# Seven VectorE operations of each parameter chain, and one product of modulations, moved to GpSimd

## The chip, the core and the metric

The kernel runs on one core of a Trainium2 chip. A core has five engines that work side by side, each through its own instructions in order: TensorE (PE, with its weight loads PEld), VectorE (DVE), ScalarE (ACT), GpSimd (POOL) and SyncE (SP, which here only issues DMA transfers; POOL issues a few too). They wait for each other by semaphores. The metric is the device time of one execution in microseconds, lower is better.

## What is computed

The reference is one block with adaptive layer norms: an S4D convolution over 2048 tokens, then a token-mixing MLP, each behind a modulated layer norm. What matters here is the S4D kernel and the modulation:

```python
dt = jnp.exp(log_dt)
A = -jnp.exp(log_A_real) + 1j * A_imag          # (D, N) = (448, 256)
C = (C_real + 1j * C_imag) * dt[:, None]
P = jnp.exp((A * dt[:, None])[:, :, None] * pos[None, None, :])
K = 2.0 * jnp.einsum("dn,dnl->dl", C, P).real   # (448, 2048)
y = irfft(rfft(u) * rfft(K))[:L]; return y + u * D_skip
...
mod = (silu(c) @ w_mod).reshape(1, 6, 1, -1)
sa, ca, ga, sb, cb, gb = (mod[:, k] for k in range(6))
h = layernorm(x) * (1 + ca) + sa
x = x + ga * S4D(h);  h = layernorm(x) * (1 + cb) + sb;  x = x + gb * MLP(h)
```

## The kernel before

**Steps.** The 448 channels go in 28 groups of 16, each group in two halves of N; one half of one group is a *step* s = 0 to 55. In a step PE makes phases (`st_phase`, line L603, into the PSUM tiles xe and xg), ACT takes absolute values and four sines of them (`st_abs` L640 and L641, `st_step` L650 to L653), GpSimd multiplies magnitudes by sines into G (L655, L656) and makes m for the step after the next (`st_mag2`, L630 and L632), DVE makes E (L657, L658, L662, L663; L662 and L663 read PSUM for the last time and so let PE's next phases go), and PE multiplies G and E into the convolution kernel (`st_kgen`, L686). Every eight steps (`BATCH`) a *window* makes the exponentials of the next eight steps at once (L614), so that ACT's tables change seldom. The order of PE, ACT, DVE and POOL is the order in which the Python code issues: there is no reordering by a scheduler.

**Work put between.** Each step calls `between()` once in its DVE work: after L658 in most steps, after L663 in steps 8 to 15 and from 32 on. It flushes held-back DVE work (L532 and L564, products out of PSUM for the transform of u), takes layer-norm statistics of x in steps 2 to 7 (`u_stats`, L503), and advances the parameter chains by `pace[s]` = 2 pieces (`more`). In the windows `more` advances them by the numbers in WPACE.

**Parameter chains.** The parameters A, C and dt are 448x256; they are prepared 128 rows at a time. The first 128 are made before the loop (`first_chain`). The rows after them are the generators `chain(q)`, q = 1, 2, 3 (the last with 64 rows): each `yield` ends a piece. The first pieces form from |C_real|/2 and |C_imag|/2 (on ACT, into xa and ya): the sum s, the difference ya, a floor under s, the reciprocal of s (into xa), the quotient ya*xa, and s scaled up where it is tiny (t, s). Then the chain yields "logs" until the next window has taken logarithms and the arctangent on ACT (`logs`, `angle`). With two pieces a step, the first pieces of chain 1 lie in steps 0 to 3, of chain 2 in 8 to 11, of chain 3 in 16 to 19; the pieces behind the logarithms lie in the windows at s = 8 and 16, and for chain 3 in the window at 24 and the steps after.

**Modulation.** mod[0] to mod[5] come from PE (L490, weights wm) and ACT (L494). In step 9 mod[0] is multiplied by mod[2] (L1070); L564 reads it from step 16 on. x and three of the weights wm are loaded by DMAs that POOL issues (L301 in steps 0 and 1, L326 in steps 2, 3 and 5), and stand in its order.

**After the steps.** From s = 32 on the pieces of the inverse transform run beside the steps; from about 404 us on two matrix products of the MLP (L1327 to L1329, L1396 to L1398) keep PE busy to the end.

Of the kernel before, what the change touches and what calls it, by code (L numbers as in the profile page):

```python
# [15 lines left out]
ALU = mybir.AluOpType  # L16
# [209 lines left out]
def tile_adaln_s4d_mixer(ctx, tc, i, out):  # L226
# [12 lines left out]
    mod = [None] * 3 + [cp.tile([P, D], F32, name=f"mod{k}") for k in range(3, 6)]  # L239
# [7 lines left out]
    with ExitStack() as es:  # L247
        V, S, G, T = nc.vector, nc.scalar, nc.gpsimd, nc.tensor
        tt, ts, stt = V.tensor_tensor, V.tensor_scalar, V.scalar_tensor_tensor
# [118 lines left out]
        def flush(todo):  # L368
            while todo:
                todo.pop(0)()  # L370

        def chain(q):


            n = min(P, D - P * q)
            cr, ci, a, aim = (raws[q][nm][0:n] for nm in ("A_C_real", "A_C_imag", "A_log_A_real", "A_A_imag"))
            xa, ya, s, t, u, ph, p64 = (
                qp.tile([P, N], F32, tag=nm, name=nm)[0:n] for nm in ("xa", "ya", "s", "t", "u", "ph", "p64")
            )

            def split(src, places):
                hl = qp.tile([P, 2, N], F32R, tag="hl", name="hl", bufs=3)[0:n]
                V.tensor_copy(hl[:, 0], src)
                yield
                tt(hl[:, 1], src, hl[:, 0].bitcast(F32), ALU.subtract)
                for k, v in places:
                    nc.sync.dma_start(pars[q][v, k, 0:n], hl.bitcast(F32))
                yield


            S.activation(xa, cr, AF.Abs, scale=0.5)
            S.activation(ya, ci, AF.Abs, scale=0.5)
            tt(s, xa, ya, ALU.add)
            yield
            tt(ya, ya, xa, ALU.subtract)
            yield
            ts(s, s, 2.0**-120, None, ALU.max)
            yield
            V.reciprocal(xa, s)
            yield  # L400
            tt(ya, ya, xa, ALU.mult)
            yield

            ts(t, s, 2.0**-40, 2.0**80, ALU.is_lt, ALU.mult)
            yield
            stt(s, t, 1.0, s, ALU.max, ALU.mult)
            yield
            tmp[q] = a, s, u, xa, ya
            while q in tmp:
                yield "logs"  # L410
            ya = u
            yield from split(a, [(0, 1), (1, 1)])
            stt(s, t, -80 * math.log(2.0) / 2.0**80, s, ALU.mult, ALU.add)
            yield
            stt(s, ya, 0.5, s, ALU.mult, ALU.add)
            yield
            ts(s, s, ldt2[0:n, q : q + 1], None, ALU.add)
            yield
            yield from split(s, [(2, 1)])
            yield "exponents"  # L420

            ts(ph, aim, dt4[0:n, q : q + 1], None, ALU.mult)
            yield
            ts(u, ph, MAGIC, MAGIC, ALU.add, ALU.subtract)
            yield
            tt(ph, ph, u, ALU.subtract)
            yield
            yield from split(ph, [(0, 0)])

            ts(u, ph, 128.0, MAGIC, ALU.mult, ALU.add)  # L430
            yield
            ts(u, u, MAGIC, None, ALU.subtract)
            yield
            stt(p64, ph, 128.0, u, ALU.mult, ALU.subtract)
            yield
            yield from split(p64, [(1, 0)])

            ts(xa, xa, 4 * i2p, -0.5, ALU.mult, ALU.add)
            yield
            ts(u, cr, 0.0, 0.5, ALU.is_ge, ALU.subtract)  # L440
            yield
            tt(xa, xa, u, ALU.mult)
            yield
            ts(u, ci, 0.0, 0.5, ALU.is_ge, ALU.subtract)
            yield
            stt(xa, xa, 0.5, u, ALU.add, ALU.mult)
            yield
            stt(xa, ph, 63.0, xa, ALU.mult, ALU.add)
            yield
            ts(u, xa, MAGIC, MAGIC, ALU.add, ALU.subtract)  # L450
            yield
            tt(xa, xa, u, ALU.subtract)
            yield
            yield from split(xa, [(2, 0)])
# [140 lines left out]
        def load(g, exps):  # L595
            load_up(g, exps)
            load_lo(g, exps)
# [445 lines left out]
        for s in range(tail):  # L1043
            if s == 32:
                early.close()
                fp = es.enter_context(tc.tile_pool(name="fp", bufs=2, reuse_waits="tile"))
                m2p.append(right("m2l", BATCH - 3))
                yks[1] = fp.tile([P, 32, DC], F32, name="yk1", bufs=1)
                for n in range(3):
                    pc_load(n)  # L1050
                t0 = fp.tile([P, 2, P], F32, name="t0", bufs=1)
                nc.sync.dma_start(t0, i["T0"].rearrange("p (j m) -> p j m", j=2))
            if s % 2 == 0 and 0 < s and s // 2 + 2 < NG:
                load(s // 2 + 2, False)
            if s == 8:
                first.close()
            if s in late:
                late[s]()
            if s < NHALF and s % BATCH == 0:
                window(s)  # L1060
                if s == 0:
                    gp_ = right("gp", 3)
            if s % BATCH == 4:
                for g in range(s // 2 + 2, min(s // 2 + 6, NG)):
                    load(g, True)

            def between():
                flush(dve)
                if s == 9:
                    tt(mod[0], mod[0], mod[2], ALU.mult)  # L1070
                if 2 <= s < BATCH:
                    for r in range(2 * s, 2 * s + 2):
                        u_stats(r)
                if s < len(pace):
                    more(pace[s])

            mellow()
            if s // BATCH == 1 or s >= NHALF:
                flush(dve)
            if s >= NHALF:  # L1080
                flush(late_act)
                flush(dve)
                mellow()
            else:
                st_abs(s)
                flush(late_act)
                if s < 32 and s % BATCH > 1:
                    st_kgen(s - 2)
                if s % BATCH == 0:
                    if s == 16:  # L1090
                        for k in (4, 5):
                            modulation(k, 0, 1)
                    elif s == 24:
                        some(u_cols, cols, 3)
                    elif s >= 32:
                        piece(False)
                if (s + 1) % BATCH:
                    st_phase(s + 1)
                elif s + 1 < NHALF:
                    st_exponents(s + 1)  # L1100

                if s > 32 and s % BATCH:
                    st_kgen(s - 1)
                st_step(s, between)
            flush(act)
            if s == NHALF:
                st_kgen(s - 1)


            if s < 2:  # L1110
                x_load(4 + 4 * s, 4 + 4 * s, G)
            free = s > 7 and not st_s1(s % BATCH == BATCH - 1)
            if s + 2 < 32 and (s + 2) % BATCH > 1:
                st_mag2(s + 2)

            if 1 < s < 8:
                modulation(s // 2, s % 2)
            if s == 7:
                par_load(2)

            if 8 <= s < 16 and free:
                some(u_rows, rows, 1)
            if s == 12:
                par_load(3)
            if s == 16:
                spec.close()
                up = early.enter_context(tc.tile_pool(name="up", bufs=3, reuse_waits="tile"))
                for n in range(4):
                    u_load(n)
            if 17 <= s < 32 and free:  # L1130
                some(u_cols, cols, 2 if s < 24 else 3)
            if s == 31:
                flush(dve)
                flush(act)
            if s > 32:
                go = pieces[0] < NP and (s % 2 == 1 or s >= NHALF)
                piece(go, None, go or s >= NHALF)
            if s == 34:

                for t in (ft, b1, b2):  # L1140
                    V.memset(t, 0.0)
                nc.sync.dma_start(ft, i["FT"])
                nc.sync.dma_start(b1, i["B_b1"].rearrange("(t p) -> p t", p=P))
                nc.sync.dma_start(b2, i["B_b2"].rearrange("(t p) -> p t", p=P))
# [164 lines left out]
    with ExitStack() as es:  # L1309
        es.enter_context(tc.manual_schedule(engines={ENG.PE, ENG.Activation, ENG.DVE, ENG.Pool}))  # L1310
        V, S, G = nc.vector, nc.scalar, nc.gpsimd
# [118 lines left out]
```

## Time and profile before

| | |
|---|---|
| median of 3 runs | 704.5 us (704.37 to 705.57) |
| the profiled execution | 708.1 us, span 705.8 us |
| busy share of the span | PE 88%, PEld 65%, DVE 65%, ACT 62%, POOL 39% |
| instructions of DVE and POOL | 877 and 326 |
| granted TensorE clock, mean | 0.956 |

The page's rows of groups give line, engine, operation, output and input names, shape and count, then busy us in total, mean ns of one, and the idle time of the engine just before them with what ended it. Timeline rows give start and length in us, engine, line and names; in brackets stands the idle time before, and what ended it. The profile of the span lists what an engine did; its waits are inferred from semaphores.

### The profile page before, as it was taken

What the parts mean: (1) busy time and instruction counts of PE and PEld (TensorE: products, weight loads), DVE (VectorE), ACT (ScalarE), POOL (GpSimd) and SP (SyncE); (2) the same over time, 40 slices, a digit from 0 to 9 for tenths busy, and PEclk for the clock granted to TensorE, in tenths of its full rate; (3) what the DMA queues carried; (4) which work ended last, traced back from release to release, by engine and by line L of the source; (5) the groups of instructions that cost most, each with busy time, mean ns of one, the idle gap of its engine ahead of it and who ended that gap; (6) DMA issues with size and microseconds to landing.
All of it is one profiled execution on the core that took longest, in us unless ns stands there. A gap on an engine that the chain in (4) does not pass through costs nothing. (4 is left out here: it accounts for less than half of the span.)

```text
span 705.8 us, 18228 instructions
## 1 busy us (share of the span) xinstructions
PE 620.8 (88%) x7164; PEld 459.6 (65%) x7164; DVE 456.3 (65%) x877; ACT 437.6 (62%) x876; POOL 271.8 (39%) x326
## 2 busy tenths in 40 slices
PE   0759878899988879788988879999999999999997
PEld 0435445445435556565665647778999999999996
DVE  7579899889678487794864468777622263344441
ACT  5838698889887799998862558878422242222220
POOL 6487468268267778887755500000000000000000
PEclk9988999999998899998898999999999999999999
DMA  7795555568795435444246889994674445555540
GB/s 173 212 186 144 200 169 171 192 214 254 236 298 171 123 77 164 122 136 139 79 125 222 256 229 249 240 203 128 186 228 138 143 130 158 157 156 157 170 130 27
DMA packets 104051, 121.69 MB, mean 172 GB/s; under 512 B 12730, under 2 KB 91758, under 8 KB 103838
## 3 DMA queue, kind: packets, MB, share of 16 engines
q1 hardware_dynamic: 102430, 113.66, 56.1%
q0 software_dynamic: 1536, 6.87, 4.4%
q8 instruction: 57, 0.93, 0.6%
q14 instruction: 28, 0.23, 0.1%
HBM read 85.14 MB, written 34.87 MB: 170 GB/s over the span
## 5 line engine op out<-in xcount | busy, mean ns | idle before, releaser
L211 ACT CAST whi<-w 128x896 fp32r<-128x896 f32 x64 | 59.9, 940 | 139.4 <-PE o L1397 84.6
L655 POOL TENSOR_TENSOR G<-mag,gs 128x512 f32<-128x512 f32 x56 | 72.0, 1285 | 76.3 <-ACT gs L651 76.3
L220 DVE TENSOR_TENSOR wlo<-w,whi 128x896 fp32r<-128x896 f32 x64 | 68.0, 1085 | 40.3 <-ACT whi L211 31.0
L603 PE MATMUL xg<-tab,lph 64*128 64x512 f32 x112 | 66.6, 596 | 20.5 <-issue 7.3
L1327 PE MATMUL acc<-h3h,whi 128*128 128x448 f32 x224 | 82.8, 370 | 0.3 <-ACT h3h L1241 0.3
L1328 PE MATMUL acc<-h3l,whi 128*128 128x448 f32 x224 | 81.6, 364 | 1.1 <-DVE h3l L1248 0.9
L1397 PE MATMUL o<-ul,whi 128*128 128x448 f32 x224 | 81.4, 363 | 0.0
L1396 PE MATMUL o<-uh,whi 128*128 128x448 f32 x224 | 81.2, 363 | 0.0
L1329 PE MATMUL acc<-h3h,wlo 128*128 128x448 f32 x224 | 80.8, 360 | 0.0
L1398 PE MATMUL o<-uh,wlo 128*128 128x448 f32 x224 | 80.7, 360 | 0.0
L686 PEld LDWEIGHTS kg<-E,G 128*32 128x32 f32 x3584 | 58.3, 118 | 34.2 <-issue 17.2
L603 PE MATMUL xe<-tab,lph 64*128 64x512 f32 x112 | 65.9, 591 | 9.7 <-ACT gs L652 7.4
L686 PE MATMUL kg<-E,G 128*32 128x64 f32 x3584 | 68.5, 232 | 5.2 <-issue 3.9
L656 POOL TENSOR_TENSOR G<-mag,gs 128x512 f32<-128x512 f32 x56 | 71.8, 1282 | 0.0
L1400 DVE SCALAR_TENSOR_TENSOR y<-o,b,mod 128x448 f32<-128x448 f32 x16 | 11.0, 685 | 80.2 <-PE o L1398 80.2
L632 POOL TENSOR_TENSOR m<-mag,w 128x512 f32<-128x512 f32 x56 | 60.0, 1071 | 6.0 <-DVE E L663 1.5
L657 DVE TENSOR_TENSOR E<-m,xe 128x512 f32<-128x512 f32 x56 | 38.1, 681 | 28.2 <-ACT xe L650 22.8
L640 ACT ACTIVATE ab<-xe 128x512 f32<-128x512 f32 x56 | 34.0, 607 | 31.8 <-PE xe L603 18.3
L1327 PEld LDWEIGHTS acc<-h3h,whi 128*128 128x128 f32 x224 | 42.1, 188 | 13.2 <-issue 3.5
L603 PE MATMUL xe<-tab,lex 64*128 64x512 f32 x56 | 32.1, 586 | 18.5 <-DMA lex<-wm 16.3
L614 ACT ACTIVATE mag<-xe 128x512 f32<-128x512 f32 x56 | 35.4, 633 | 15.3 <-PE xe L603 4.4
L1328 PEld LDWEIGHTS acc<-h3l,whi 128*128 128x128 f32 x224 | 42.1, 188 | 3.8 <-DVE h3l L1248 1.2
(235 smaller groups left out, 1474.1 us busy)
## 6 DMA issues: line engine op xcount, KB each, us to landing
w<-in_B_w_dram SPq DMA_DIRECT2D x64, 224.0 KB
w<-in_B_w_dram SPq DMA_DIRECT2D x32, 448.0 KB
yu_d<-yt SPq DMA_DIRECT2D x16, 448.0 KB
yi<-yu_d SPq DMA_DIRECT2D x16, 448.0 KB
us_d<-uo SPq DMA_DIRECT2D x16, 448.0 KB
u<-us_d SPq DMA_DIRECT2D x32, 224.0 KB
v_d<-vt SPq DMA_DIRECT2D x32, 224.0 KB
vt<-v_d SPq DMA_DIRECT2D x14, 448.0 KB
```

The lines of the kernel that those rows point to most:

```text
L220: eng.tensor_tensor(lo, w, hi.bitcast(F32), ALU.subtract)
L603: T.matmul(out[k], lhs[r], rhs[r], start=start, stop=stop)
L632: G.tensor_tensor(m2, me, w[:, :, None].to_broadcast([P, GD, 32]), ALU.mult)
L655: G.tensor_tensor(Gt[:, 1], mg_, v32(sg), ALU.mult)
L656: G.tensor_tensor(Gt[:, 0], mg_, v32(cg_), ALU.mult)
L686: T.matmul(kgs[g][32 * q : 32 * q + 32, m], Gt[:, c, d], E[:, c, d], start=h == 0 and c == 0 and m == 0, stop=h == 1 and c == 1, skip_grou ...
L1327: nc.tensor.matmul(acc[f], hi[:, fs], h3h[:, r], start=r == 0, stop=False)
L1328: nc.tensor.matmul(acc[f], hi[:, fs], h3l[:, r], start=False, stop=False)
L1329: nc.tensor.matmul(acc[f], lo[:, fs], h3h[:, r], start=False, stop=r == 15)
L1396: nc.tensor.matmul(o, hi[:, ks], uh[kh][:, k], start=kh == 0 and k == 0, stop=False)
L1397: nc.tensor.matmul(o, hi[:, ks], ul[kh][:, k], start=False, stop=False)
L1398: nc.tensor.matmul(o, lo[:, ks], uh[kh][:, k], start=False, stop=kh == 1 and k == 6)
```

## The change

Of the first pieces of `chain(q)`, all but the reciprocal are issued to GpSimd instead of VectorE. The fused last piece becomes two (GpSimd does a maximum into u, then a product), and one empty piece is put in front of the reciprocal, so that a chain has two pieces more ahead of its logarithms. The product of modulations in step 9 goes to GpSimd too. In the changed kernel lines behind the chain have numbers higher by 3.

```diff
-            tt(s, xa, ya, ALU.add)
+            G.tensor_tensor(s, xa, ya, ALU.add)
             yield
-            tt(ya, ya, xa, ALU.subtract)
+            G.tensor_tensor(ya, ya, xa, ALU.subtract)
             yield
-            ts(s, s, 2.0**-120, None, ALU.max)
+            G.tensor_scalar(s, s, 2.0**-120, None, ALU.max)
+            yield
             yield
             V.reciprocal(xa, s)
             yield
-            tt(ya, ya, xa, ALU.mult)
+            G.tensor_tensor(ya, ya, xa, ALU.mult)
             yield
-            ts(t, s, 2.0**-40, 2.0**80, ALU.is_lt, ALU.mult)
+            G.tensor_scalar(t, s, 2.0**-40, 2.0**80, ALU.is_lt, ALU.mult)
             yield
-            stt(s, t, 1.0, s, ALU.max, ALU.mult)
+            G.tensor_scalar(u, t, 1.0, None, ALU.max)
+            yield
+            G.tensor_tensor(s, u, s, ALU.mult)
             yield
...
                 if s == 9:
-                    tt(mod[0], mod[0], mod[2], ALU.mult)
+                    G.tensor_tensor(mod[0], mod[0], mod[2], ALU.mult)
```

What this does to the orders is seen at two places. GpSimd in steps 0 to 3 before (the transfers of x and of the weights wm_79 stand between G and m; a number at a name's end tells tiles apart):

```order
L656 TENSOR_TENSOR G<-mag,gs 128x512
L301 DMA xt<-in_A_u_dram 32x1792 x4
L630 TENSOR_TENSOR w<-mag 128x16
L632 TENSOR_TENSOR m_417<-mag,w 128x512
L655 TENSOR_TENSOR G<-mag,gs 128x512
L656 TENSOR_TENSOR G<-mag,gs 128x512
L301 DMA xt<-in_A_u_dram 32x3584 x4
L630 TENSOR_TENSOR w<-mag 128x16
L632 TENSOR_TENSOR m_454<-mag,w 128x512
L326 DMA wm_79<-in_w_mod_dram 112x4x448
L655 TENSOR_TENSOR G<-mag,gs 128x512
L656 TENSOR_TENSOR G<-mag,gs 128x512
```

and GpSimd at the same place after it, from the first added operation to the product that needs the reciprocal:

```order
L393 TENSOR_TENSOR s<-xa,ya 128x256
L395 TENSOR_TENSOR ya<-ya,xa 128x256
L301 DMA xt<-in_A_u_dram 32x1792 x4
...
L397 TENSOR_SCALAR s<-s 128x256
L301 DMA xt<-in_A_u_dram 32x3584 x4
...
L326 DMA wm_79<-in_w_mod_dram 112x4x448
L658 TENSOR_TENSOR G<-mag,gs 128x512
L659 TENSOR_TENSOR G<-mag,gs 128x512
L402 TENSOR_TENSOR ya<-ya,xa 128x256
L633 TENSOR_TENSOR w<-mag 128x16
L635 TENSOR_TENSOR m_528<-mag,w 128x512
```

The first x transfers stand behind two added operations, the second behind three; L402 (L401 before) stands between G of step 2 and everything of step 3.

DVE in steps 9 and 10 before, with the product of modulations and the third to sixth piece of chain 2 (L532 is a product for u, out of PSUM):

```order
L662 TENSOR_TENSOR E<-mag,xg 128x16x32
L663 TENSOR_TENSOR E<-m_1041,xg 128x16x32
L1070 TENSOR_TENSOR mod_104<-mod_104,mod_106 128x448
L397 TENSOR_SCALAR s<-s 128x256
L399 RECIPROCAL xa<-s 128x256
L532 TENSOR_TENSOR yt<-pu,mod_105 128x448 x2
L657 TENSOR_TENSOR E<-m_1280,xe 128x16x32
L658 SCALAR_TENSOR_TENSOR E<-mag,xe 128x16x32
L662 TENSOR_TENSOR E<-mag,xg 128x16x32
L663 TENSOR_TENSOR E<-m_1280,xg 128x16x32
L401 TENSOR_TENSOR ya<-ya,xa 128x256
L404 TENSOR_SCALAR t<-s 128x256
```

and DVE there after it:

```order
L665 TENSOR_TENSOR E<-mag,xg 128x16x32
L666 TENSOR_TENSOR E<-m_1042,xg 128x16x32
L535 TENSOR_TENSOR yt<-pu,mod_105 128x448 x2
L660 TENSOR_TENSOR E<-m_1281,xe 128x16x32
L661 SCALAR_TENSOR_TENSOR E<-mag,xe 128x16x32
L665 TENSOR_TENSOR E<-mag,xg 128x16x32
L666 TENSOR_TENSOR E<-m_1281,xg 128x16x32
L400 RECIPROCAL xa<-s 128x256
```

Between the steps' own work only the reciprocal is left, one step later than before.

## Prediction

> **What bounds the kernel now.** I read the page first, for where VectorE (DVE) and GpSimd (POOL) are busy; the busy share of 40 slices of 17.6 us each:
>
> ```profile
> DVE  7579899889678487794864468777622263344441
> ...
> POOL 6487468268267778887755500000000000000000
> ```
>
> The diff touches steps s=0 to 4, 8 to 12 and 16 to 20 of the channel loop, which lie at 31 to 54, 95 to 115 and 147 to 165 us (slices 2 to 10). GpSimd is no idle engine there: its digits are 8, 7, 4, 6, 8, 2, 6, 8, 2. What comes after 180 us only inherits the time at which these steps end.
>
> Next the groups by line, for what leaves DVE. Columns: busy us in total and mean ns of one, then idle before.
>
> ```profile
> L399 DVE RECIPROCAL xa<-s 128x256 f32<-128x256 f32 (+1 forms) x3 | 5.2, 1750 | 0.1
> L401 DVE TENSOR_TENSOR ya<-ya,xa 128x256 f32<-128x256 f32 (+1 forms) x3 | 5.0, 1653 | 0.0
> L393 DVE TENSOR_TENSOR s<-xa,ya 128x256 f32<-128x256 f32 (+1 forms) x3 | 2.9, 972 | 1.6 <-ACT ya L392 1.6
> L404 DVE TENSOR_SCALAR t<-s 128x256 f32<-128x256 f32 (+1 forms) x3 | 2.8, 937 | 0.0
> L406 DVE SCALAR_TENSOR_TENSOR s<-t,s 128x256 f32<-128x256 f32 (+1 forms) x3 | 1.4, 470 | 0.0
> L397 DVE TENSOR_SCALAR s<-s 128x256 f32<-128x256 f32 (+1 forms) x3 | 1.4, 466 | 0.0
> L1070 DVE TENSOR_TENSOR mod<-mod,mod 128x448 f32<-128x448 f32 x1 | 1.3, 1335 | 0.0
> L395 DVE TENSOR_TENSOR ya<-ya,xa 128x256 f32<-128x256 f32 (+1 forms) x3 | 1.3, 442 | 0.1
> ```
>
> All but the reciprocal leave: 5.0+2.9+2.8+1.4+1.4+1.3+1.3 = 16.1 us of DVE. That is more than the work is worth: L395 needs 0.44 us for what L401 needs 1.65. The timeline shows why:
>
> ```profile
> 45.88 3.37 DVE L401 TENSOR_TENSOR ya<-ya,xa 128x256 f32<-128x256 f32 x1
> ...
> 47.69 1.26 POOL L656 TENSOR_TENSOR G<-mag,gs 128x512 f32<-128x512 f32 x1
> ```
>
> L401 ends (49.25) 0.3 us after GpSimd's product (48.95): a DVE operation whose inputs all lie in SBUF stands still while GpSimd works. So each of the three places has to be asked which engine is late there.
>
> **Steps 0 to 4 (31 to 60 us).**
>
> ```profile
> 32.00 2.00 POOL L301 DMA_DIRECT2D xt<-in_A_u_dram  x4
> 41.18 0.76 POOL L326 DMA_DIRECT2D wm<-in_w_mod_dram  x1
> ...
> 44.39 0.63 DVE L503 BATCH_NORM_STATS2 st<-xt 128x6 f32<-128x448 f32 x1 [4.73 <-DMA xt<-in_A_u_dram]
> 50.01 0.68 DVE L663 TENSOR_TENSOR E<-m,xg 128x512 f32<-128x512 f32 x1
> ...
> 43.27 0.60 ACT L651 ACTIVATE gs<-xg 128x512 f32<-128x512 f32 x1 [1.45 <-POOL G L655]
> 54.02 0.60 ACT L651 ACTIVATE gs<-xg 128x512 f32<-128x512 f32 x1
> ...
> 50.79 0.76 PE L603 MATMUL xg<-tab,lph 64*128 64x512 f32 x1 [7.26 <-issue]
> ...
> 58.62 0.30 PEld L490 LDWEIGHTS pm<-wm,scb 112*128 112x128 f32 x2 [0.35 <-DMA wm<-in_w_mod_dram]
> ```
>
> DVE waits for x until 44.39, goes through two statistics, L401 (3.37) and L404, and PE starts the next phases as L663 ends, at 50.7. But PE then comes to the modulation at 58.62 and waits there for weights that GpSimd's queue issued at 41.18. What this place is worth is therefore bounded by that transfer.
>
> **What it costs on GpSimd.** No such operation of 256 columns stands on GpSimd in this place; the nearest rows:
>
> ```profile
> L791 POOL TENSOR_TENSOR z<-zx,zy 128x224 f32<-128x224 f32 x28 | 18.6, 664 | 29.2 <-DVE zy L789 24.8 <-DVE ks L705 2.2 <-PE kg L686 1.3
> L519 POOL TENSOR_SCALAR xt<-xt,rs,nm 128x448 f32<-128x448 f32 x6 | 4.7, 788 | 3.0 <-DVE nm L512 3.0
> L845 POOL TENSOR_TENSOR wm<-A_log_A_real,wm 128x256 fp32r<-128x256 f32 x1 | 0.7, 718 | 0.1
> L844 POOL CAST wm<-A_log_A_real 128x256 fp32r<-128x256 f32 x1 | 0.4, 396 | 1.9 <-ACT A_log_A_real L863 1.9
> ```
>
> Successive GpSimd instructions overlap by 0.05 us. A two-input operation: between 0.62 (L791, 224 columns) and 0.73; I take 0.67, L845 with the same 256 columns. A one-input operation: between 0.35 (L844, 256 columns) and 0.74 (L519, 448 columns); I take 0.47, nearer L844, which has the same columns but less arithmetic. The modulation product (448 columns): 1.0 to 1.28, what L632 and L655 take for 512 columns in the rows of steps 8 to 15 below; I take 1.1. A chain has four of the first and three of the second (the fused L406 becomes two): 4x0.67 + 3x0.47 = 4.1 us, against 4.9 us that it took on DVE on average, waits included ((16.1-1.3)/3). I price the third chain, with 64 rows, like the others, so GpSimd gets 3x4.1+1.1 = 13.4 us.
>
> In the table "Engine selection" (section 4.1) of GPSIMD Engine Reference, the Trainium skill puts elementwise work on VectorE and calls GpSimd about twice as slow for two inputs; L845 against L395 is 718 to 442 ns, 1.6 times. Twice 0.44 would be 0.88 for each two-input operation, an estimate that adds 0.8 us to each chain and would take the sum below from -0.7 to about +0.1.
>
> **Steps 0 to 4, the change.** On DVE, L401 and L404 (45.88 to 49.4) go, and the reciprocal, postponed a step, comes there (1.66 from start to start): L663 would end 1.9 us earlier. Against it, the x transfers at 32.00 now stand behind two added operations (2x0.67 = 1.3 us); I let them land 1.0 later, so L663 ends 0.9 earlier, and PE and ACT follow by as much. The new wait is on GpSimd: the product L401 waits for that reciprocal until 48.6, and m, a weight issue and the two G of step 3 queue behind it, the first ending near 52.6, the second near 53.9 instead of 48.95. ACT's L651 of step 4, which waits for the first of them as the row at 43.27 does, stands at 54.02-0.9 = 53.1: covered by 0.5 us. Were that gone, PE's wait for the weights covers 0.9 us more. PE meets the weights at 58.6 either way. Their queue is never empty from 32 us on, so what the later issue loses is what other transfers gain meanwhile: I take +0.2, with -0.35 (the wait vanishes) and +1.3 (every transfer slips by the issue) as ends.
>
> **Steps 8 to 15.** Columns of the first row: stretch, length, then busy us of PE, PEld, DVE, ACT, POOL, and clock, DMA share, GB/s.
>
> ```profile
> 104.00:110.00 6.00, 4.14 (x77) 2.28 (x77) 6.00 (x10) 5.47 (x12) 5.84 (x7) 1.00 0.72 212
> ...
> 94.42 1.28 POOL L655 TENSOR_TENSOR G<-mag,gs 128x512 f32<-128x512 f32 x1 [12.67 <-ACT gs L651]
> 102.72 1.27 POOL L655 TENSOR_TENSOR G<-mag,gs 128x512 f32<-128x512 f32 x1
> 106.51 1.27 POOL L655 TENSOR_TENSOR G<-mag,gs 128x512 f32<-128x512 f32 x1
> 113.51 1.05 POOL L632 TENSOR_TENSOR m<-mag,w 128x512 f32<-128x512 f32 x1
> 116.79 1.29 POOL L655 TENSOR_TENSOR G<-mag,gs 128x512 f32<-128x512 f32 x1 [2.23 <-ACT gs L651]
> ...
> 114.63 0.60 ACT L640 ACTIVATE ab<-xe 128x512 f32<-128x512 f32 x1 [2.13 <-PE xe L603]
> 119.51 0.60 ACT L651 ACTIVATE gs<-xg 128x512 f32<-128x512 f32 x1
> 124.79 0.63 ACT L653 ACTIVATE xg<-ab 128x512 f32<-128x512 f32 x1
> 126.90 0.68 DVE L663 TENSOR_TENSOR E<-m,xg 128x512 f32<-128x512 f32 x1
> 127.72 0.47 PE L603 MATMUL xg<-tab,lex 64*128 64x512 f32 x1 [0.73 <-DVE ks L705]
> 134.21 0.60 ACT L614 ACTIVATE mag<-xe 128x512 f32<-128x512 f32 x1 [0.77 <-PE xe L603]
> ```
>
> Here DVE is the bound: it has no gap, ACT waits 2.13 us for phases that DVE's late L663 let go. But GpSimd has no gap either from 94.42 to 114.5. Its bare step is 3.79 us (102.72 to 106.51); five took 20.1 instead of 19.0, so 1.1 us of waiting for DVE's SBUF operations vanish with them. It gets 4.1+1.1 = 5.2 us. So G of step 13 starts at 114.55+5.2-1.1 = 118.7 instead of 116.79 and ends at 119.95. ACT's L651 of step 14 waits for this G, as at 43.27, so it moves from 119.51 to 120.0. ACT runs without a gap from there: L653 of step 15 ends at 125.85 instead of 125.35. DVE, now early, follows with two products at once: L663 ends at 127.2 instead of 127.58, and PE's next exponents start then. So the 5.8 us taken from DVE give back 0.4 us: the bound goes from DVE to GpSimd's order. With the ends of the prices (4.5 to 6.4 us on GpSimd) this is -1.1 to +0.8. That ACT is 0.5 late is hidden in the next window, in the 0.77 us of the last row.
>
> The Trainium skill's SBUF — State Buffer (section "SBUF: two separate sides") says that the port pair of DVE and GpSimd is locked for a whole instruction and the loser blocks; the rows of L401 agree. Without such a lock GpSimd would not get its 1.1 us back, and this place would be an estimated +0.7.
>
> **Steps 16 to 23.**
>
> ```profile
> 152.19 2.98 PE L557 MATMUL pu<-yi,s 128*128 128x448 f32 x4 [0.19 <-DMA yi<-yu_d]
> 160.36 0.50 PE L603 MATMUL xe<-tab,lph 64*128 64x512 f32 x1
> 161.07 0.46 PE L603 MATMUL xg<-tab,lph 64*128 64x512 f32 x1 [0.21 <-ACT xg L653]
> ...
> 160.30 0.67 DVE L663 TENSOR_TENSOR E<-m,xg 128x512 f32<-128x512 f32 x1
> ```
>
> From 152.19, when yi lands, PE has nearly no gap to 177; it loses only the 0.7 us before 161.07, when L663 of step 18 ended (160.97). After the change that L663 ends near 159.6. GpSimd gets 4.1 us and runs up to 1.4 late, and has caught up at its gap before step 23. So -0.5, ends -0.65 and +0.3.
>
> **Sum.** +0.2-0.4-0.5 = -0.7 us. The profiled execution took 708.1 (span 705.8), 3.6 above the median 704.5; it would become 707.4, and the median 703.8. The ends add up to -2.1 and +2.4.
>
> **The rivals.**
> 1. *GpSimd becomes the bound outright (slower).* Two-input operations at 0.88 (twice L395), one-input ones at 0.74, the product 1.28: 5.7+1.3-1.1 = 5.9 us net in steps 8 to 12 instead of 4.1, so that place costs 1.4 instead of gaining 0.4; the weights slip by 1.3; steps 16 to 23 give nothing. Sum +2.7: 707.2. It decides from 4.5 us net on. For it: GpSimd's gapless 20 us. Against: 2.23 us of gap at 116.79 and L845's price.
> 2. *DVE's release comes through (faster).* If GpSimd's lateness does not reach ACT, ACT's gap of 2.13 us goes, and 0.35 and 0.65 in the other two places: -3.1, 701.4. For it: DVE is the gapless engine that all wait for. Against: L651 depends on G.
> 3. *Nothing arrives.* The transfers (weights at 58.6, yi at 152.2) fix the times: 704.5, within the case of the forecast.
>
> **How the numbers follow.** About 0.2% (1.4 us) is what a measurement of this kernel can tell from no change. Forecast, with rival 3: 0.43, its own range 702.4 to 706.9, from the ends. Rival 1: 0.25. Rival 2: 0.32. Hence faster 0.32, same 0.43, slower 0.25. The range reaches to both rivals' times, 701.4 to 707.2.
>
> **What would show it.** Right: DVE's 16.1 us gone and gaps of DVE in steps 9 to 15; GpSimd two-input operations near 0.7; ACT's L651 (now L654) of steps 11 to 14 waiting for GpSimd; G of step 3 about 5 us later; PE still waiting for the weights near 58.6. Wrong: GpSimd operations of 1 us or more; ACT without waits for GpSimd in steps 11 to 14; the weights landing more than 1 us later; or a part after 180 us whose length changes.

## The result, and the profile after

The changed kernel takes 712.1 us (median of 13 runs, 708.74 to 718.04) against 704.5 of the kernel before on the same chip: ratio 1.0104, 95% interval 1.0078 to 1.0131. It is 7.6 us slower, above the predicted range. The profiled execution took 711.2 us, its span 709.4. One profile used further down (the idle work, first dose) fell in an execution with a low granted clock (0.934); only its steps 0 to 6 are read.

The page after, the same two rows of 40 slices as before, and the granted clock:

```profile
DVE  7563889788769768695864558777622263344441
POOL 6496629829729878879765400000000000000000
PEclk9866997899999989899998999999999999999999
```

DVE's fourth slice (53 to 71 us) has a 3 where it had a 9, and the clock row a 6 in the third and fourth, where the page before has an 8 in both (a second execution of the changed kernel has an 8 and a 7). DVE's busy time on the page is 444.2 us after 456.3, GpSimd's 287.4 after 271.8: 16.1 us of work left DVE, but its busy time fell by 12.1 only.

The groups of the changed kernel for what now runs on GpSimd (busy us, mean ns of one | idle before):

```profile
L405 POOL TENSOR_SCALAR t<-s 128x256 f32<-128x256 f32 (+1 forms) x3 | 3.2, 1083 | 0.0
L407 POOL TENSOR_SCALAR u<-t 128x256 f32<-128x256 f32 (+1 forms) x3 | 2.6, 851 | 0.2
L397 POOL TENSOR_SCALAR s<-s 128x256 f32<-128x256 f32 (+1 forms) x3 | 2.5, 847 | 0.0
L402 POOL TENSOR_TENSOR ya<-ya,xa 128x256 f32<-128x256 f32 (+1 forms) x3 | 2.2, 731 | 0.0
L395 POOL TENSOR_TENSOR ya<-ya,xa 128x256 f32<-128x256 f32 (+1 forms) x3 | 2.2, 730 | 0.2
L409 POOL TENSOR_TENSOR s<-u,s 128x256 f32<-128x256 f32 (+1 forms) x3 | 2.2, 729 | 0.0
L393 POOL TENSOR_TENSOR s<-xa,ya 128x256 f32<-128x256 f32 (+1 forms) x3 | 2.2, 724 | 0.0
L1073 POOL TENSOR_TENSOR mod<-mod,mod 128x448 f32<-128x448 f32 x1 | 1.1, 1149 | 0.0
```

Operations with two tile inputs take 0.73 us, those with one take more: 0.85, 0.85 and 1.08. A chain is 4 x 0.73 + 2.78 = 5.7 us, not 4.1.

Steps 0 to 7, the timeline of the kernel before, and behind it that of the changed kernel:

```profile
37.84 2.00 POOL L301 DMA_DIRECT2D xt<-in_A_u_dram  x4
52.78 3.35 PE L490 MATMUL pm<-wm,scb 112*128 112x448 f32 x4
58.62 1.77 PE L490 MATMUL pm<-wm,scb 112*128 112x448 f32 x4
60.32 1.10 PE L686 MATMUL kg<-E,G 128*32 128x64 f32 x64
62.62 0.60 ACT L640 ACTIVATE ab<-xe 128x512 f32<-128x512 f32 x1 [0.45 <-PE xg L603]
90.82 0.64 ACT L640 ACTIVATE ab<-xe 128x512 f32<-128x512 f32 x1
125.57 0.46 ACT L473 ACTIVATE xa<-ya 128x256 f32<-128x256 f32 x1
```

```profile
40.48 2.03 POOL L301 DMA_DIRECT2D xt<-in_A_u_dram  x4
43.41 0.63 DVE L506 BATCH_NORM_STATS2 st<-xt 128x6 f32<-128x448 f32 x1 [4.86 <-DMA xt<-in_A_u_dram]
43.85 0.77 POOL L326 DMA_DIRECT2D wm<-in_w_mod_dram  x1
44.90 1.72 DVE L400 RECIPROCAL xa<-s 128x256 f32<-128x256 f32 x1
47.08 0.73 POOL L402 TENSOR_TENSOR ya<-ya,xa 128x256 f32<-128x256 f32 x1
60.59 0.63 DVE L506 BATCH_NORM_STATS2 st<-xt 128x6 f32<-128x448 f32 x1 [7.73 <-DMA xt<-in_A_u_dram]
62.82 3.35 PE L493 MATMUL pm<-wm,scb 112*128 112x448 f32 x4 [6.34 <-DMA wm<-in_w_mod_dram]
66.10 1.94 PE L689 MATMUL kg<-E,G 128*32 128x64 f32 x64
69.87 0.60 ACT L643 ACTIVATE ab<-xe 128x512 f32<-128x512 f32 x1 [1.40 <-PE xg L606]
98.05 0.63 ACT L643 ACTIVATE ab<-xe 128x512 f32<-128x512 f32 x1
134.82 0.44 ACT L476 ACTIVATE xa<-ya 128x256 f32<-128x256 f32 x1
```

The second transfer of x, x(1) (the first row of each), is issued 2.64 us later than before, the weights behind it 2.67 later. x(1) lands so late that DVE stands for 7.73 us until 60.59, the weights follow 2.2 us later, and PE, long ready, waits 6.34 us for them: its products begin 4.20 us later than before. Then the same four products take 3.35 us instead of 1.77 and the next kg 1.94 instead of 1.10, another 2.4 us: the granted clock is 0.50 from 62 to 68 us, where the kernel before had 1.00 from 58 to 62. The kernel before has such a place too, a little earlier: at 52.78 four products of the same kind take 3.35 us, behind PE's pause of 7.26 us that the prediction shows at 50.79. ACT's Abs of step 6 comes at 69.87 instead of 62.62, 7.25 us late, of which landing and clock explain 6.6.

From the Abs of step 8 (at 90.82 before, at 98.05 after) to the arctangent behind step 15 (the last row of each) it was 34.75 us and is 36.77: another 2.0 lost. What ACT waits for there, in the changed kernel:

```profile
118.47 0.60 ACT L654 ACTIVATE gs<-xg 128x512 f32<-128x512 f32 x1 [0.74 <-POOL G L658]
124.27 0.60 ACT L654 ACTIVATE gs<-xg 128x512 f32<-128x512 f32 x1 [1.41 <-POOL G L658]
128.74 0.60 ACT L654 ACTIVATE gs<-xg 128x512 f32<-128x512 f32 x1 [1.10 <-POOL G L658]
```

Three times, in steps 12 to 14, it waits for GpSimd's G of the step before, 3.25 us in all. What happens after 180 us cannot be read from this pair of profiles: stretches of both, before first:

```profile
200.00:250.00 50.00, 41.50 (x765) 24.61 (x761) 36.38 (x63) 39.37 (x77) 36.75 (x42) 0.86 0.59 182
```

```profile
200.00:250.00 50.00, 43.55 (x782) 24.83 (x784) 41.07 (x70) 42.67 (x82) 38.11 (x44) 0.97 0.74 228
```

The granted clock was 0.86 there in the one and 0.97 in the other. From the Abs of step 24 to that of step 32 the fourteen profiles of this case take 45.9 to 53.3 us, without an order by kernel. So places are read from traces up to step 23, and what arrives at the end from the medians.

### The profile page after: what moved, and what is told of

Same layout as the page of the kernel before. It is cut to its first block, busy times and chain, and to the rows that moved or that the text cites. A ratio compares the mean times of both kernels' runs of the same rounds, so it can differ in the third digit from the quotient of the medians.

```text
span 709.4 us, 18232 instructions
## 1 busy us (share of the span) xinstructions
PE 621.6 (88%) x7164; PEld 458.9 (65%) x7164; DVE 444.2 (63%) x858; ACT 438.1 (62%) x876; POOL 287.4 (41%) x348
## 5 line engine op out<-in xcount | busy, mean ns | idle before, releaser
L689 PEld LDWEIGHTS kg<-E,G 128*32 128x32 f32 x3584 | 60.4, 120 | 36.6 <-issue 14.4
L689 PE MATMUL kg<-E,G 128*32 128x64 f32 x3584 | 71.0, 236 | 6.0 <-ACT ks L703 2.4
L1399 PEld LDWEIGHTS o<-uh,whi 128*128 128x128 f32 x224 | 42.1, 188 | 3.4
```

Of the source, the lines that this page charges most:

```text
L689: T.matmul(kgs[g][32 * q : 32 * q + 32, m], Gt[:, c, d], E[:, c, d], start=h == 0 and c == 0 and m == 0, stop=h == 1 and c == 1, skip_grou ...
L1399: nc.tensor.matmul(o, hi[:, ks], uh[kh][:, k], start=kh == 0 and k == 0, stop=False)
```

## The experiments

Two theories went in. The *transfer theory*: chain 1 on GpSimd stands ahead of the transfers that GpSimd issues, the claimed weights land late, PE waits and loses its clock; nearly all of the 7.6 us is that. The *work theory*: the moved computations themselves are late, in all three places.

**Chain 1 back on VectorE** (chains 2 and 3 and the product as changed).

```diff
-            G.tensor_tensor(s, xa, ya, ALU.add)
...
+            if q > 1:
+                G.tensor_tensor(s, xa, ya, ALU.add)
...
+            else:
+                tt(s, xa, ya, ALU.add)
...
```

> The changed kernel, but chain 1 (steps 0 to 4) has its operations on VectorE again; chains 2 and 3 and the product of modulations stay on GpSimd. Transfer theory (the three added operations ahead of the x and weight transfers in GpSimd's order delay the weights on which TensorE stands near 58 us, and its clock falls meanwhile): the 7 us of steps 5 to 6 vanish, about +1.5 us to the kernel before (1.002), the rest being steps 8 to 23. Work theory (GpSimd is simply loaded with too much, each of the three chains costs alike): two thirds of the loss stay, about +5 us (1.007).

Measured: 706.19 us against 706.04, ratio 1.0010 (0.9973 to 1.0047). The loss is gone when a third of the moved work is taken back. ACT's Abs of step 6 is at 63.31.

**Chain 1 alone on GpSimd**, all else as before (the same branch with `q == 1`, in the kernel before).

> The kernel before, but chain 1 alone has its seven operations on GpSimd. Transfer theory: +6 to +7 us (1.009), TensorE waits for the weights near 57 to 63 us as in the changed kernel. Work theory: a third of the loss, +2.5 us (1.0035).

Measured: 712.37 us, ratio 1.0097 (1.0060 to 1.0134). A third of the work makes the whole loss. Abs of step 6 is at 68.72, 6.1 us late.

**The changed kernel with its chains from step 2 on**, so that nothing stands ahead of the transfers of x.

```diff
-        pace = [2] * 32
+        pace = [0, 0] + [2] * 30
```

> The changed kernel with one number edit: no chain piece in steps 0 and 1, so chain 1 begins in step 2, behind both x transfers and the first weights in GpSimd's order; the same operations are on GpSimd. Transfer theory: weights land near 58 to 59 us as in the kernel before, TensorE keeps its clock, +0 to +2 us (1.001). Work theory: GpSimd does as much in the same steps 0 to 7, nothing changes, +7.5 us (1.0105).

Measured: 707.41 us, ratio 1.0025 (0.9987 to 1.0063). All three chains are on GpSimd, and about three quarters of the loss are gone.

```profile
37.81 2.00 POOL L301 DMA_DIRECT2D xt<-in_A_u_dram  x4
58.65 3.27 PE L493 MATMUL pm<-wm,scb 112*128 112x448 f32 x4 [2.74 <-DMA wm<-in_w_mod_dram]
```

Issue and landing are those of the kernel before (37.84 and 58.62). PE comes to the weights earlier than there, waits 2.74 us, and its products are slow.

**The changed kernel reading the late weights later**: the products of modulations 2 and 3 move to steps 6 and 7.

```diff
-            if 1 < s < 8:
-                modulation(s // 2, s % 2)
+            for k, h in {2: [(1, 0)], 3: [(1, 1)], 6: [(2, 0), (2, 1)], 7: [(3, 0), (3, 1)]}.get(s, []):
+                modulation(k, h)
```

> The changed kernel, but the modulation products of the weights that land late are made on TensorE in steps 6 and 7 instead of 4 to 7 (same products, read two steps later). Transfer theory: the transfers land as late as in the changed kernel, but TensorE does not stand for the weights; it then waits for VectorE, which stands for x until about 60.6, so 3 to 4.5 us of the 7.5 come back: +3 to +4.5 us (1.005). Work theory: nothing comes back, +7.5 us.

Measured: 708.65 us, ratio 1.0039 (1.0003 to 1.0074). GpSimd's work and the issue of the transfers stay as changed; taking away PE's wait for the weights gives some 4.5 us back (+- 3 by the two intervals). DVE still waits for x(1) until 60.44, and Abs of step 6 is 2.4 us late (65.03).

**Idle work ahead of the transfers**, in the kernel before: the delay without the change.

```diff
                 flush(dve)
+                if s < 2:
+                    im = raws[1]["A_A_imag"]
+                    idle = qp.tile([P, N], F32, tag="p64", name="p64")
+                    if s == 0:
+                        for _ in range(2):
+                            G.tensor_tensor(idle, im, im, ALU.add)
+                    else:
+                        G.tensor_scalar(idle, im, 2.0**-120, None, ALU.max)
```

> The kernel before, with three operations added on GpSimd whose results nobody reads: two additions of 128x256 in step 0 and one maximum in step 1 (some 2.3 us by the rows of the changed kernel), ahead of the issue of the transfer of x(1). No work leaves VectorE. Transfer theory: the three set the issue of x(1) and of the claimed weights wm(2) back by some 2.3 us, the weights land 2 to 4 us later, PE waits for them and runs on at the lower clock: +4 to +7 us, ratio 1.006 to 1.010, ScalarE's Abs of step 6 some 5 to 7 us late. Work theory (the time comes from the moved computations, whose results are late): nothing waits for these three, so 0 to +0.7 us, ratio 1.000 to 1.001.

Measured: 708.03 us against 704.59, ratio 1.0035 (0.9996 to 1.0073). That is below the +4 to +7 us expected, and the time alone does not decide: the interval takes in no change. The trace shows the chain of events:

```profile
40.54 2.04 POOL L301 DMA_DIRECT2D xt<-in_A_u_dram  x4
61.54 3.35 PE L490 MATMUL pm<-wm,scb 112*128 112x448 f32 x4 [4.44 <-DMA wm<-in_w_mod_dram]
```

Issue 2.70 us later, weights 2.92 later, half clock behind PE's wait (granted 0.50 from 61 to 65 us), and Abs of step 6 4.97 us late (67.59). So the dose was doubled (`range(4)`, and two maxima):

> The kernel before with twice the idle work of the earlier run: four additions of 128x256 in step 0 and two maxima in step 1 on GpSimd, some 5 us ahead of the issue of the transfer of x(1); no work leaves VectorE. The first dose moved the issue by 2.7 and the landing of the weights by 2.9 us and the run by 0 to 5 (ratio 1.0035). Transfer theory: issue +5.3, PE's products with the claimed weights at 63.5 to 65 (58.62 before), ScalarE's Abs of step 6 +7 to +9, the run +5 to +8 us, ratio 1.007 to 1.011. If the landing did not depend on the issue, or the wait were covered later: ratio below 1.004.

Measured: 711.28 us against 704.82, ratio 1.0078 (1.0046 to 1.0110). Work that nobody needs makes most of the changed kernel's loss, though with an issue delayed by 4.72 us, 1.8 times the changed kernel's 2.64; at nearly the same delay (the first dose, 2.70) it made 2.5 us by the ratio, with no change inside the interval.

```profile
42.56 2.04 POOL L301 DMA_DIRECT2D xt<-in_A_u_dram  x4
62.13 3.35 PE L490 MATMUL pm<-wm,scb 112*128 112x448 f32 x4 [9.83 <-DMA wm<-in_w_mod_dram]
```

The landing at 62.13 was expected at 63.5 to 65 and Abs of step 6 came 5.8 late, not 7 to 9: an issue 4.72 later made the weights only 3.51 later. Why is seen in the DMA's share (last column but one) from 34 to 44 us, in the kernel before, in the changed one and in this one, of which one stretch of 2 us is shown besides:

```profile
34.00:44.00 10.00, 9.38 (x148) 5.68 (x148) 5.63 (x9) 5.48 (x12) 9.80 (x13) 1.00 0.91 198
```

```profile
34.00:44.00 10.00, 7.57 (x142) 4.49 (x141) 3.45 (x6) 5.18 (x10) 9.81 (x16) 0.77 0.79 178
```

```profile
34.00:44.00 10.00, 9.05 (x148) 5.54 (x148) 7.59 (x14) 4.95 (x10) 9.74 (x15) 0.72 0.52 129
...
40.00:42.00 2.00, 2.00 (x7) 0.68 (x4) 0.00 (x0) 1.97 (x5) 1.92 (x3) 1.00 0.21 48
```

The DMA engines move less while GpSimd is late with the next issue: a share of 0.91 before, 0.79 after, 0.52 with the doubled dose, down to 0.21 just ahead of the issue of x(1). One reading, which no run tests, is that what they don't move there comes later, and that a part is given back because less is in flight when x(1) is issued: from the issue of x(1) to the start of the products with the weights it is 20.8 us before, 22.3 in the changed kernel, 21.0 and 19.6 with the two doses.

**PE kept at work while it waits**: how much of the loss is the clock.

```diff
                 pmods[k] = pms.tile([P, D], F32, tag="ms", name="pm")
+                for _ in range(28 if k == 2 else 0):
+                    T.matmul(pmods[k], mg[:, 0], ones[:, 0:D], start=True, stop=True)
```

> The changed kernel, with 28 more bf16 products of 128x448 on PE ahead of the claimed weights' products of modulation 2, so that PE does work while it waits for the weights (their results are overwritten). The landing of the weights stays late. If the lower clock after the wait carries some 3 us of the 7 (four products in 3.35 us where they had taken 1.77, kg's in 1.94 instead of 1.10): the four products come back to about 1.8 us, and the run to some 4 us over before, ratio 1.005 to 1.007. If the late landing alone carries the loss and the clock's part is taken up by later slack: ratio 1.009 to 1.011, as the changed kernel. Were the added products themselves in the way: above 1.011.

```profile
55.58 5.47 PE L492 MATMUL pm<-ones,mg 128*128 128x448 bf16 x28
61.82 1.77 PE L495 MATMUL pm<-wm,scb 112*128 112x448 f32 x4 [0.77 <-DMA wm<-in_w_mod_dram]
63.52 1.10 PE L691 MATMUL kg<-E,G 128*32 128x64 f32 x64
```

In the trace it worked: with a wait of 0.77 us the four products take 1.77 and kg 1.10, at full clock, and Abs of step 6 is 3.2 us late instead of 7.25. The Trainium skill (TensorE: Matmul & The Clock Gate, "Part 1: The HAM clock gate") says that one idle window of about 3.4 us halves PE's clock; that agrees with half clock behind waits of 4.44, 6.34 and 9.83 us and full clock behind 0.77. But less was enough in three runs: behind waits of 2.51, 2.63 and 2.74 us (the two-input run, the next run, the chains from step 2) the four products took 3.17, 3.06 and 3.27 us. Nor did the full clock show in the time: it was 712.31 us, ratio 1.0105 (1.0062 to 1.0148, 6 runs). So the kernel was run again beside the changed kernel:

> The run with the 28 added products once more, beside the changed kernel itself on the same chip, since its first interval (1.0062 to 1.0148) held both answers. Half clock as a part of the loss: 2 to 4 us below the changed kernel of this job. Late landing alone: within 1.5 us of it.

> The changed kernel as it is, for the comparison with the run that keeps PE at work: +5.5 to +9 us over before, ratio 1.008 to 1.013, by either reading.

Measured: 709.09 us, ratio 1.0057 (1.0027 to 1.0086), and the changed kernel 711.75, ratio 1.0080 (1.0050 to 1.0111). The means of 12 runs each lie 2.5 us apart, with a deviation of 2.4 within each, so 2.5 +- 2.1. In this profile the 28 products were over before the weights came (PE waited another 2.63 us and ran on at a lower clock, 3.06 and 1.43 us for the four products and kg), so it tests the full clock only in part. The first run gives no sign that anything arrives at the end (1.0105, where the changed kernel had 1.0104), the second says 0.4 to 4.6 us: the clock's share of the final time stays open, the fact of the half clock does not.

**Only the operations with two tile inputs on GpSimd**, chains from step 2 on, and the **kernel before with its chains from step 2 on** as the control.

```diff
-            G.tensor_scalar(s, s, 2.0**-120, None, ALU.max)
-            yield
+            ts(s, s, 2.0**-120, None, ALU.max)
 ...
-            G.tensor_scalar(t, s, 2.0**-40, 2.0**80, ALU.is_lt, ALU.mult)
-            yield
-            G.tensor_scalar(u, t, 1.0, None, ALU.max)
+            ts(t, s, 2.0**-40, 2.0**80, ALU.is_lt, ALU.mult)
             yield
-            G.tensor_tensor(s, u, s, ALU.mult)
+            stt(s, t, 1.0, s, ALU.max, ALU.mult)
```

> Of the change only the operations with two tile inputs stay on GpSimd (the sum, the difference, the product with the reciprocal, and the product of modulations); the maximum, the comparison and the fused product go back to VectorE in their old form; and the chains are issued from step 2 on. GpSimd then has 3 x 0.73 = 2.2 us a channel in place of some 5.7, VectorE is 1.0 to 1.3 us a channel lighter than before. Transfer theory with the second loss of steps 8 to 15 put down to GpSimd's one-input operations: x(1) is issued as before, ScalarE no longer waits for G in steps 8 to 15, and the run ends between -2 us and 0, ratio 0.997 to 1.000. If the second loss has to do with VectorE's operations waiting for GpSimd's results rather than with GpSimd's load: as the changed kernel with its chains from step 2 on, ratio 1.0025 or more.

> The kernel before with only the issue of the channels' chains held back to step 2 (all on VectorE as before): the control of the runs that hold them back. Nothing of GpSimd's moves; VectorE's operations of chain 1 come a step or two later. Both theories: 0 to +0.7 us, ratio 1.000 to 1.001. More than +1.4 us would say that a part of what the held back variants of the changed kernel lose lies in the later start of the chains and not on GpSimd.

Measured: 706.45 us, ratio 1.0011 (0.9979 to 1.0042); the control 706.38, ratio 1.0026 (0.9990 to 1.0063). The control was expected at 0 to +0.7 us and came at +1.8. So the run of all three chains from step 2 on, at 1.0025, lost nothing that can be measured against its own control, and starting the chains late is no cure in itself. The two-input kernel came 0.1% above what was expected of it, and its interval takes in no change. ACT was expected to wait for no G in steps 8 to 15 and still waited twice (0.25 and 1.17 us); PE waited 2.51 us for the weights, as in the first run with chains from step 2 on.

**Chain 1 back, and of chains 2 and 3 only the two-input operations on GpSimd.**

> Chain 1 all on VectorE as before; of chains 2 and 3 only the three operations with two tile inputs on GpSimd, the maximum, the comparison and the fused product on VectorE; the product of modulations on GpSimd. The transfers of x are then issued as before, and GpSimd gets 2.2 us a channel and 1.15 for the product in steps 8 to 15, less the 1.1 that it no longer waits. If GpSimd's slow one-input operations carry the loss of steps 8 to 23 that the traces showed in the run with only chain 1 back (ScalarE's arctangents of step 15 +2.8, of step 23 +5.3): arctangents of step 15 at 0 to +1, and the run at -2 to 0 us, ratio 0.997 to 1.000. If those shifts were a matter of the granted clock and not of GpSimd: no difference from the run with chain 1 back, ratio 1.000 to 1.002.

Measured: 702.23 us against 704.82, ratio 0.9955 (0.9922 to 0.9987). It is 2.6 us below the kernel before in the medians, the only run whose interval lies below 1, and 9.5 us below the changed kernel (711.75, measured beside it). That is more than the -2 to 0 us expected. ACT's arctangent of step 15 comes at 124.71, 0.86 earlier than before. Transfers and weights are as before (x(1) issued at 38.22, products at 58.90 behind a wait of 0.22), and in steps 8 to 15 one wait of ACT for GpSimd is left:

```profile
110.81 0.60 ACT L668 ACTIVATE gs<-xg 128x512 f32<-128x512 f32 x1 [0.85 <-POOL G L672]
```

With only chain 1 back, and the one-input operations of chain 2 still on GpSimd, there were three:

```profile
111.99 0.60 ACT L671 ACTIVATE gs<-xg 128x512 f32<-128x512 f32 x1 [1.12 <-POOL G L675]
117.79 0.60 ACT L671 ACTIVATE gs<-xg 128x512 f32<-128x512 f32 x1 [1.41 <-POOL G L675]
122.28 0.60 ACT L671 ACTIVATE gs<-xg 128x512 f32<-128x512 f32 x1 [1.11 <-POOL G L675]
```

Over the thirteen other profiles, from the Abs to the arctangent of the same eight steps, us:

| on GpSimd of the chain whose pieces stand there (chain 2, chain 3) | profiles | steps 8 to 15 | steps 16 to 23 |
|---|---|---|---|
| nothing | 4 | 33.95 to 34.76 | 34.79 to 35.51 |
| all but the reciprocal, and the product of modulations | 7 | 36.75 to 36.84 | 35.59 to 36.26 |
| the three two-input operations, and that product | 2 | 33.60 and 33.61 | 34.58 and 34.61 |

The groups don't overlap. All but the reciprocal costs 2.0 to 2.9 us in steps 8 to 15 and 0.1 to 1.5 in steps 16 to 23; the two-input operations alone gain a little there, by two profiles. Between the last two rows lie the 2.8 us of one-input operations in a chain, and with them the product of the fused piece (0.73) and the extra pieces, which went back too: 3.5 us of GpSimd's time decide the place, four fifths of it one-input operations. No run takes the one-input operations back alone. That these differences arrive whole at the end is not shown: chain 1 back, with 2.1 us lost in steps 8 to 15, was timed at 1.0010.

## Why the prediction was wrong

**Steps 0 to 4 (+0.2, ends -0.35 and +1.3): the step that failed.** "PE meets the weights at 58.6 either way. Their queue is never empty from 32 us on, so what the later issue loses is what other transfers gain meanwhile." PE met them at 62.82, and the DMA engines do move less between GpSimd's issues, as the shares of the stretches show. Three errors are in it. The upper end took the two additions ahead of the first transfer of x, 1.3 us; ahead of the second one and of the weights stand three operations, and the issue moved by 2.64. The weights slipped by 1.56 more than their issue, 4.20 in all; why by so much, where the first idle dose made 2.92 of 2.70, stays open. And the term ended at the landing: it left out that PE, idle for 6.34 us, runs on at half clock (2.4 us), though the trace before had the same at 52.78. Measured at the Abs of step 6: +7.25; in the end, by chain 1 alone, +6.8 us (ratio 1.0097). The forecast's own signs of being wrong named this: weights more than 1 us later, and a GpSimd operation of over 1 us (L405, 1.08). The new wait that this part did price, GpSimd's L402 waiting for the reciprocal until 48.6, did not occur; L402 ran at 47.08 without a gap. The prediction let x(0), the first transfer of x, land 1.0 us later; issued 1.84 us later (33.84 after 32.00), it came 0.98 us earlier (43.41 after 44.39), so DVE was through with the reciprocal by 46.6, and PE's next phases started 2.9 us earlier than before (47.85 after 50.79), not 0.9. That lead was lost again in the wait for the weights.

**Steps 8 to 15 (-0.4, ends -1.1 and +0.8): mechanism right, size and so sign wrong.** ACT waits for G, as predicted, but for that of steps 11, 12 and 13 and by 3.25 us in all, where the prediction had step 13 alone and 0.5. The mis-sized term is the one-input price: 0.47 us taken, from a cast; 0.85, 0.85 and 1.08 measured, above even the upper end of 0.74. The two-input price (0.67 against 0.73) and the product (1.1 against 1.15) held. GpSimd gets 5.7 + 1.15 - 1.1 = 5.75 us net (the trace has 5.65: G of step 13 starts 25.78 us after that of step 8, before it took 20.13 without the gap), and the place costs +2.0 instead of gaining 0.4. Rival 1 named 4.5 us net as the point of decision and 1.4 as the cost: its mechanism, somewhat larger. That its 5.9 us net came so near is luck in part: it had the two-input operations too dear (0.88) and the one-input ones too cheap (0.74). In GPSIMD Engine Reference, section 4.1, the Trainium skill gives two-input work as the slow kind on GpSimd and one input as "roughly line-rate"; the trace has it the other way round (0.73 us against 0.85 to 1.08).

**Steps 16 to 23 (-0.5, ends -0.65 and +0.3).** +0.8 in this pair, with the same mis-sized term; by the table between 0.1 and 1.5.

**Rival 2 (DVE's release comes through, -3.1).** Its condition, that GpSimd's lateness does not reach ACT, was not met by this change. Where it nearly was, with chain 1 back and the two-input operations alone, the run was faster by 0.1 to 0.8% (ratio 0.9955). By this one run the release is worth about that much; that the gain is DVE's release is argued from the shorter steps 8 to 23 (33.6 and 34.6 us in the table), not tested alone. The rest of the change spent it three times over.

**What a measurement can tell.** The prediction took 0.2% for this; the intervals here are +- 0.26 to 0.43%, so runs expected within 0.2% of each other could not be told apart.

## What to carry to other kernels

Before work is given to an engine with time to spare, list the DMA issues in its queue: each moves back by about the work put ahead of it (2.3 us of it made 2.64 here), and if a matrix engine waits for what they fetch, it stands until the landing and can run on at half clock; how much of the latter arrives at the end stayed open here. Price a moved operation from the same kind of operation on the new engine: a cast is no measure of a maximum or a comparison.

## What was not expected of the hardware

On GpSimd a maximum with a constant over 128x256 floats takes 0.85 us and a comparison with a multiplication 1.08, more than a product of two tiles (0.73). On DVE the same maximum took 0.47 on average in the kernel before.

An issue that is 2.6 to 2.7 us late made its data 2.9 us late in one kernel and 4.2 in another, and one 4.7 us late only 3.5: the delay of the issue alone does not give that of the landing. For x(0) it is even the other way round in all fourteen profiles: issued at 32.0 to 33.0 us (six of them) it landed at 44.2 to 46.8, issued at 33.4 to 35.0 (eight) at 42.2 to 43.8. That what else is in flight decides is a guess; no run tests it.

A pause of PE of 2.6 us was enough to halve its clock: in the second run with the added products the granted clock was 1.00 from 56 to 62 us, and 0.53 from 63 to 65 behind the wait of 2.63 us.
